# The first block of transposed x: two plain loads turned by TensorE instead of one, and the weight loads on one queue

## The chip, the cores and the metric

The kernel runs on one core of one Trainium2 chip. The metric is the device time of one execution in microseconds (us). One run in the set was taken with the hardware profiler; its trace gives every instruction with its start, its length and what it waited for, and the packets and landings of the DMAs.

## What is computed

The input x has 2048 rows (the sequence, S) of 512 columns (D), in bfloat16. Two mixers work on it, and a gate blends them:

```
g = sigmoid((x * gate_w).sum(-1))                       # one number a row
qkv = x @ wqkv                                          # 512 -> 3 * 512: q, k, v, 32 heads of 16
logits[s, w] = q[s] . k[s - 2 w] / 4,  w = 0..7         # sliding, dilated by 2; s - 2 w < 0 is masked
a = (softmax(logits) @ v[s - 2 w]) @ wo
h = layernorm(x)
b = (gelu(h^T @ w1 + b1) @ w2 + b2)^T                   # an MLP along the sequence: 2048 -> 1792 -> 2048
out = g * a + (1 - g) * b
```

What matters here is the very start: the product x @ wqkv, which needs x with its columns on the partitions, that is x transposed, and the layer norm, which needs x as it is.

## The kernel before, in words

**Layout.** x is kept twice. `X` holds it as it is, 16 tiles of 128 rows. `XT` holds it transposed: 4 parts of 128 columns (index d), each with 2048 entries along the sequence, which is worked on in 4 blocks of 512 rows. `WQKV` holds the weights as 4 parts of 128 rows (again d) by 1536 columns, q first, then k, then v. One projection is one of q, k, v for 128 of its 512 columns (index dl) and one block of 512 rows: four products, one for each d, that add up in one bank of PSUM (`f_proj`, line 614, products at L619). ScalarE copies the finished bank to SBUF (`f_evq`, L627 for q, L630 for k and v).

**The first block.** The eight projections of block 0 (q and k, four dl each) use all eight PSUM banks at once, and they are issued not projection by projection but part by part, as the parts of x and of the weights come in (the loop at lines 635 to 641): d = 0 of the four q, then d = 1, 2, 3 of the four q, then d = 0 and 1 of the four k, then d = 2 and 3 of the four k. So there are 32 products in a row, and then block 1 follows, q and k in turn, one projection after the other.

**How the transposed x arrives.** Three of the four parts of block 0 (384 columns) and all of the other blocks come by a transposing DMA (`ld_xt0`, L473, and `ld_xt`, L460). Part d = 0 of block 0 comes by a plain load of 512 rows by 128 columns (`d_xp`, line 479, issued through the helper at L429) into a borrowed buffer, `OUTS`. TensorE turns it by four products of 128 columns with an identity matrix (`f_tr`, L545), two of them into bank 5, two into bank 6; ScalarE copies bank 5 to `XT` (L555) and VectorE bank 6 (L557). The first four projections' products can start after both copies.

**Warm-up.** While the first loads are under way, TensorE multiplies constants (`f_warm`, L537): six products of 512 columns and one of 256 ahead of the turn, and one of 512 behind it.

**Queues.** SyncE (SP) issues nearly all loads, in the order of the program, ScalarE's queue (ACT) two of the first weight loads. Before: SP issues d_xp, the transposing DMA of 384 columns, the q weights for d = 2 and d = 3, the k weights for d = 0 and 1, those for d = 2 and 3, x tiles 0 and 1 (x0), the transposing DMA of block 1 (xt1), then x tiles 2 and 3 (x2), 4 to 7 (x4), blocks 2 and 3 (xt2, xt3), x8, x12, the v weights and the MLP's weights. ACT issues the q weights for d = 0 and d = 1. From x2 on, a load waits for the fifth load before it (`throttle`).

**Order of the work.** The kernel is planned when it is built: `_Sched` (line 72) simulates the engines with costs given by hand and fixes the order of each engine's instructions. For the first nine loads the time at which they are taken to land is written in by hand (`op_.lands`, line 487). The products of the projections are held in their order by `last_main`. VectorE's order is written out by hand (the `chain` at line 959): the indicator `rp`, the copy `ev_trb`, the layer norm's statistics of tiles 0 to 3 (`ln1_*`, L574), then the first products of q with shifted k (`qkm_0_0_0`, L690), and so on. The sums of those products over a head's columns are TensorE's, in two bursts of 64 products (`qkr_*`, L698). At the end of the kernel TensorE makes a @ wo (L878) and VectorE combines (L899).

## Time and profile before

| | |
|---|---|
| three runs | 167.96, 168.19, 168.55 us; median 168.19 us |
| the profiled execution | 168.55 us, its span 167.3 us |
| TensorE products | 860, busy 163.9 us (98% of the span) |
| VectorE | busy 151.3 us (90%) |
| ScalarE | busy 75.0 us (45%) |
| SyncE's DMA queue (q1) | 24.85 MB, 54.0% of 16 engines' span |
| ScalarE's DMA queue (q10) | 4.66 MB, 10.0% |
| first loads, from issue to landing | d_xp 3.1 us; q weights on ACT 3.0 us (median of two); transposing DMA of 384 columns 4.4 us; 128 KB weight loads on SP 3.0 us |

The span runs from the first instruction of the program to its last; the time of a run has 1.25 us more, which lie around the span. In the lists below, a line begins with start and length in us, or with a window; then come the engine (PE is TensorE's products, PEld its weight loads, DVE VectorE, ACT ScalarE, SP SyncE), the line of the kernel, the operation, what it writes and reads, its shape and how many such instructions were merged; in brackets, the idle time ahead of it and what ended it. `arena` is the whole of the kernel's SBUF, `ps` its PSUM. A product's shown length includes its way through the array, so products overlap: the pace is read from start to start.

### The profile page before, as it was taken

The page shows a single profiled execution, that of the slowest core. Times are in us where ns is not written, and L with a number is a line of the kernel's source. Part 1 is how long each engine was busy: PE and PEld are TensorE (multiplying, and loading weights), DVE is VectorE, ACT ScalarE, POOL GpSimd, SP SyncE. Part 2 cuts the span into 40 slices and gives each one's busy share as a digit, 9 for nine tenths or more (in the row PEclk, how much of TensorE's full clock was granted, in tenths as well). Part 3 has the DMA queues.
Part 4 walks back from the last instruction along what each step waited for, and adds up shares of the span by engine and source line. Part 5 has one row for each costly group of instructions (what it writes and reads, how often), then busy time and mean ns, then how long its engine had stood idle before and what let it go on. Part 6 is the DMA issues. An engine that isn't in the chain of part 4 may idle for free.

```text
span 167.3 us, 2152 instructions
## 1 busy us (share of the span) xinstructions
PE 163.9 (98%) x860; PEld 77.6 (46%) x860; DVE 151.3 (90%) x154; ACT 75.0 (45%) x116; POOL 0.7 (0%) x8
## 2 busy tenths in 40 slices
PE   7999999999999999999999999999999999999994
PEld 2455555554454444444444444444444444444463
DVE  0145999999999999999999999999999999999896
ACT  3077688889899818793113121131231321310100
POOL 1000000000000000000000000000000000000000
DMA  5999999968003837996579936462672580000454
GB/s 130 315 272 262 303 322 291 307 196 246 0 0 97 311 115 187 303 290 153 133 183 343 335 129 143 112 187 68 184 218 83 138 223 0 0 0 0 157 190 159
DMA packets 47625, 29.64 MB, mean 177 GB/s; under 512 B 9856, under 2 KB 46464, under 8 KB 47616
## 3 DMA queue, kind: packets, MB, share of 16 engines
q1 hardware_dynamic: 45504, 24.85, 54.0%
q10 hardware_dynamic: 2112, 4.66, 10.0%
q8 instruction: 7, 0.11, 0.3%
q14 instruction: 2, 0.02, 0.0%
HBM read 21.24 MB, written 2.10 MB: 140 GB/s over the span
## 4 chain that ended last, share of the span: by engine, by line
PE 94%; DVE 3%; DMA 2%; issue 0%
PE ps L812 29%; PE ps L862 29%; PE ps L619 25%; PE ps L878 6%; PE ps L698 4%; DVE arena L899 2%; DMA arena<-in_A_x_dram 2%; PE ps L545 0%; DVE arena L557 0%
## 5 line engine op out<-in xcount | busy, mean ns | idle before, releaser
L812 PE MATMUL ps<-arena 128*128 128x512 bf16 x224 | 48.7, 379 | 0.0
L862 PE MATMUL ps<-arena 128*128 128x512 bf16 x224 | 48.7, 379 | 0.0
L619 PE MATMUL ps<-arena 128*128 128x512 bf16 x192 | 42.3, 382 | 0.1
L690 DVE TENSOR_TENSOR arena<-arena 128x4096 bf16<-128x4096 bf16 (+1 forms) x12 | 35.5, 2996 | 2.3 <-ACT arena L630 1.8
L797 DVE TENSOR_TENSOR arena<-arena 128x8192 bf16<-128x8192 bf16 x8 | 35.0, 4419 | 0.0
L812 PEld LDWEIGHTS ps<-arena 128*128 128x128 bf16 x224 | 21.8, 98 | 26.7 <-ACT arena L728 0.4
L862 PEld LDWEIGHTS ps<-arena 128*128 128x128 bf16 x224 | 21.9, 98 | 26.5
L619 PEld LDWEIGHTS ps<-arena 128*128 128x128 bf16 x192 | 21.6, 114 | 20.8 <-DVE arena L557 0.7
L930 ACT ACTIVATE arena<-ps,arena 128x512 bf16<-128x512 f32 x16 | 12.4, 778 | 39.4 <-PE ps L862 39.4
L800 DVE TENSOR_TENSOR arena<-arena 128x4096 bf16<-128x4096 bf16 (+1 forms) x16 | 27.0, 1752 | 0.0
L630 ACT ACTIVATE arena<-ps 128x512 bf16<-128x512 f32 x32 | 18.5, 596 | 4.5 <-PE ps L619 4.5
L833 ACT ACTIVATE arena<-ps,arena 128x512 bf16<-128x512 f32 x14 | 9.6, 687 | 22.2 <-PE ps L812 17.4
L574 DVE BATCH_NORM_STATS2 arena<-arena 128x6 f32<-128x512 bf16 x16 | 10.0, 680 | 5.6 <-DMA arena<-in_A_x_dram 5.6
L878 PE MATMUL ps<-arena 128*128 128x512 bf16 (+1 forms) x80 | 14.2, 337 | 0.0
L899 DVE SCALAR_TENSOR_TENSOR arena<-ps,arena 128x512 bf16<-128x512 f32 (+1 forms) x20 | 11.5, 638 | 0.9 <-PE ps L878 0.7
L598 ACT ACTIVATE arena<-arena 128x512 bf16<-128x512 bf16 x16 | 12.2, 806 | 0.0
L627 ACT ACTIVATE arena<-ps 128x512 bf16<-128x512 f32 x16 | 9.0, 596 | 5.5 <-PE ps L619 5.4
L878 PEld LDWEIGHTS ps<-arena 128*128 128x128 bf16 x80 | 7.8, 98 | 6.3
L674 DVE SCALAR_TENSOR_TENSOR arena<-arena 128x512 bf16<-128x512 bf16 x16 | 10.1, 685 | 0.0
L744 DVE TENSOR_TENSOR arena<-arena 128x512 bf16<-128x512 bf16 (+4 forms) x11 | 7.3, 667 | 0.6 <-ACT arena L763 0.2
L698 PE MATMUL ps<-arena 128*32 128x512 bf16 x128 | 7.3, 380 | 0.0
L728 ACT ACTIVATE arena<-ps 128x512 bf16<-128x512 f32 x8 | 4.7, 592 | 4.6 <-PE ps L698 4.6
(42 smaller groups left out, 40.5 us busy)
## 6 DMA issues: line engine op xcount, KB each, us to landing
arena<-in_B_w_dram SPq DMA_DIRECT2D x7, 1024.0 KB, 8.3
arena<-in_B_w_dram SPq DMA_DIRECT2D x8, 896.0 KB, 5.1
arena<-arena ACTq DMA_DIRECT2D x32, 128.0 KB, 3.0
arena<-in_A_x_dram SPq DMA_DIRECT2D x4, 512.0 KB, 5.1
out_dram<-arena SPq DMA_DIRECT2D x14, 128.0 KB, 1.7
arena<-in_A_x_dram SPq DMA_DIRECT2D x1, 1536.0 KB, 7.9
arena<-in_A_wqkv_dram SPq DMA_DIRECT2D x2, 256.0 KB, 3.6
arena<-in_A_x_dram SPq DMA_DIRECT2D x2, 256.0 KB, 3.5
```

Of the source, the lines that this page charges most:

```text
L598: A("act", (lambda t_: (lambda e: e.activation(out=X[:, t_, :], in_=X[:, t_, :], func=AF.Identity, scale=col(RSTD, t_), bias=col(NMR, t_)) ...
L619: ins = e.matmul(ps[:, bank, s0:s1], lhsT=lhsT, rhs=XT[:, dt, sb * 512 + s0:sb * 512 + s1], start=(dt == 0 and s0 == 0), stop=(dt == 3))
L630: return lambda e: e.activation(out=dst, in_=ps[:, bank, :], func=AF.Copy)
L690: return lambda e: e.tensor_tensor(out=PBL[buf][:, :, 512 * c0:512 * (c0 + nc_)], in0=in0, in1=in1, op=ALU.mult)
L698: ins = e.matmul(ps[32 * c:32 * c + 32, 4 + wl, :], lhsT=RP, rhs=PBL[buf][:, wl, c * 512:(c + 1) * 512], start=(dl == 0), stop=(dl == 3), ...
L797: A("dve", (lambda o_, i0, i1: (lambda e: e.tensor_tensor(out=o_, in0=i0, in1=i1, op=ALU.mult)))(pv, in0, in1), 4.4, reads=v_res + ["atx_% ...
L800: A("dve", (lambda pv_, n__: (lambda e: e.tensor_tensor(out=pv_[:, 0:n__], in0=pv_[:, 0:n__], in1=pv_[:, n__:2 * n__], op=ALU.add)))(pv, n ...
L812: ins = e.matmul(ps[:, bank, :], lhsT=W1W[:, slot, st, 128 * e_:128 * e_ + 128], rhs=X[:, st, :], start=(st == 0), stop=(st == NST - 1))
L862: ins = e.matmul(ps[:, bank, :], lhsT=W2S[slot][:, ft, 128 * e_:128 * e_ + 128], rhs=UT[:, ft, :], start=(ft == 0), stop=(ft == NFT - 1))
L878: ins = e.matmul(ps[:, bank, 0:c1 - c0], lhsT=OT[:, t, 128 * i:128 * i + 128], rhs=WO[:, t, c0:c1], start=(t == 0), stop=(t == 3))
L899: A("dve", (lambda i_, b_, c0_, c1_: (lambda e: e.scalar_tensor_tensor(out=T1[:, i_, c0_:c1_], in0=ps[:, b_, 0:c1_ - c0_], scalar=col(G, i ...
L930: A("act", (lambda i_, bank_: (lambda e: e.activation(out=T1[:, i_, :], in_=ps[:, bank_, :], func=AF.Identity, scale=col(OMG, i_), bias=co ...
```

## The change

Two of the four parts of block 0 now come by plain loads. The borrowed buffer holds both (`xp0`, `xp1`), the second turn uses the same two banks, and its four products and two copies stand between the products of q for d = 0 and those of k for d = 0. The transposing DMA takes the other two parts, 256 columns instead of 384.

SP now issues all of the first loads: xp0, q weights for d = 0, k weights for d = 0, xp1, q and k weights for d = 1 in one load, the transposing DMA, q and k weights for d = 2, those for d = 3, xt1, and x0 behind xt1 instead of ahead of it. ACT issues none of them.

The order of the 32 products becomes: q d = 0 (4), the second turn, k d = 0 (4, in the bank order 4, 7, 5, 6), q and k d = 1 (8), q d = 2 (4), q d = 3 (4), k d = 2 and 3 (8). The warm-up is five products of 512 columns and one of 256 ahead of the first turn, and one of 512 and one of 256 behind it. VectorE's chain gets the second copy, `ev_trb1`, right behind the first. The planner's landing times are rewritten for the new loads.

```diff
-        XT0 = ["xt0_%d" % d for d in range(4)] + ["xt0_0b"]
+        XT0 = ["xt0_%d" % d for d in range(4)] + ["xt0_0b", "xt0_1b"]
...
-            dst = XT[:, 1:4, 0:512]
-            op = sch.dma("sp", lambda e: e.dma_start_transpose(dst, x2d[0:512, 128:512]), 512 * 384 * 2, ds, issue=1.25,
-                         writes=XT0[1:4], after=prev_dma(), name="d_xt0")
+            dst = XT[:, 2:4, 0:512]
+            op = sch.dma("sp", lambda e: e.dma_start_transpose(dst, x2d[0:512, 256:512]), 512 * 256 * 2, ds, issue=1.25,
+                         writes=XT0[2:4], after=prev_dma(), name="d_xt0")
...
-        XP = view("OUTS", BF16, [(128, 4), (1, 128)])
-        d_xp = sch.dma("sp", mk_dma(XP, xv[:, 0:4, 0:128]), 512 * 128 * 2, sch.dsem("xp"), writes=["outs0"], issue=0.4, name="d_xp")
...
-        first_loads = [ld_w(0, 0, 1, "act"), ld_xt0(), ld_w(0, 1, 1, "act"), ld_w(0, 2, 1), ld_w(0, 3, 1), ld_w(1, 0, 2), ld_w(1, 2, 2),
-                       ld_x(0, 2)]
+        XP = view("OUTS", BF16, [(512, 2), (128, 4), (1, 128)])
+
+        def ld_xp(dt):
+            op = sch.dma("sp", mk_dma(XP[:, dt], xv[:, 0:4, 128 * dt:128 * dt + 128]), 512 * 128 * 2, sch.dsem("xp%d" % dt),
+                         writes=["outs%d" % dt], after=prev_dma(), issue=0.4, name="d_xp%d" % dt)
+            init_dmas.append(op)
+            return op
+
+        def ld_qk(d):
+            ds = sch.dsem("wqk%d" % d)
+            op = sch.dma("sp", mk_dma(WQKV[:, d, 0:2 * D], wqkv_v[:, d, 0:2 * D]), 2 * 128 * D * 2, ds,
+                         writes=["wqkv0_%d" % d, "wqkv1_%d" % d], after=prev_dma(), issue=0.45, name="d_wqk%d" % d)
+            init_dmas.append(op)
+            return op
+
+        first_loads = [ld_xp(0), ld_w(0, 0, 1), ld_w(1, 0, 1), ld_xp(1), ld_qk(1), ld_xt0(), ld_qk(2), ld_qk(3)]
         ld_xt(1)
         first_loads.append(init_dmas[-1])
+        first_loads.append(ld_x(0, 2))
...
+        def turn(dt, prev):
+            for h in range(2):
+                lgr = ["lg%d_0" % (5 + h), "lg%d_1" % (5 + h)]
+                prev = A("pe", f_tr(dt, h), 0.215 if dt == 0 else 0.11, reads=["outs%d" % dt, "ident"], writes=lgr, after=[prev],
+                         name="tr%d%d" % (dt, h), prio=-100 if dt == 0 else 0)
+                dst = XT[:, dt, 256 * h:256 * h + 256]
+                pin = ps[:, 5 + h, 0:256]
+                if h == 0:
+                    A("act", (lambda d_, i_: (lambda e: e.activation(out=d_, in_=i_, func=AF.Copy)))(dst, pin), 0.35,
+                      reads=lgr, writes=["xt0_%d" % dt], name="ev_tra%d" % dt, prio=0)
+                else:
+                    A("dve", (lambda d_, i_: (lambda e: e.tensor_copy(out=d_, in_=i_)))(dst, pin), 0.35,
+                      reads=lgr, writes=["xt0_%db" % dt], name="ev_trb%d" % dt, prio=0)
+            return prev
...
-        A("pe", f_warm(6), 2.56, writes=["lg7_0", "lg7_1"], name="warm1", prio=-100)
+        A("pe", f_warm(5), 2.13, writes=["lg7_0", "lg7_1"], name="warm1", prio=-100)
...
+        w3_ = A("pe", f_warm(1, 256), 0.2, writes=["lg7_0", "lg7_1"], after=[tr_], name="warm4", prio=-100)
...
-        for (b0, d0, d1, s0, s1) in ((0, 0, 1, 0, 512), (0, 1, 2, 0, 512), (0, 2, 3, 0, 512), (0, 3, 4, 0, 512), (4, 0, 2, 0, 512), (4, 2, 4, 0, 512)):
-            for b in range(b0, b0 + 4):
+        for (bs, d0, d1, s0, s1) in ((range(4), 0, 1, 0, 512), ((4, 7, 5, 6), 0, 1, 0, 512), (range(8), 1, 2, 0, 512),
+                                     (range(4), 2, 3, 0, 512), (range(4), 3, 4, 0, 512), (range(4, 8), 2, 4, 0, 512)):
+            if bs == (4, 7, 5, 6):
+                last_main[0] = turn(1, last_main[0])
+            for b in bs:
...
-        chain(["rp", "ev_trb"] + ln1(0, 1, 2, 3) + ["qkm_0_0_0", "qkm_0_1_0"] + ln1(4, 5, 6, 7) + ln2(0)
+        chain(["rp", "ev_trb0", "ev_trb1"] + ln1(0, 1, 2, 3) + ["qkm_0_0_0", "qkm_0_1_0"] + ln1(4, 5, 6, 7) + ln2(0)
```

21 lines of the change are left out of this document (6 added, 15 removed).

## The prediction, on record before the changed kernel ran

> **What bounds the kernel now.** I read the chain that ended last first, then the first microseconds in order of time, then VectorE's waits, then the DMA rates of the first five microseconds. The chain in order of time (start, length, what):
>
> ```profile
> 0.80 3.10 DMA arena<-in_A_x_dram
> ...
> 4.04 0.60 PE ps L545 x4
> ...
> 4.66 0.44 DVE arena L557
> ...
> 5.15 33.44 PE ps L619 x152
> ...
> 161.68 3.98 DVE arena L899 x9
> ```
>
> From 5.15 us on the chain is TensorE alone, without a wait, up to the last output columns: 152 products in 33.44 us are 0.22 us each, and the tail behind TensorE (the last combine and its store) is the same whatever happens at the start. The 860 products are the time; only what lies ahead of 5.15 us, and work added to TensorE, can move the end. Ahead of it stands one path: the load d_xp (issued 0.80, landed 3.91), four small products that turn it (L545), ScalarE's and VectorE's copies of the result (L555, L557), then the first projection at 5.15, that is 1.24 us after the landing.
>
> TensorE's pace in these microseconds, by its weight loads in order of time:
>
> ```profile
> 2.07 0.15 PEld L537 LDWEIGHTS ps<-const-bfloat16-1.0 128*128 128x128 bf16 x1 [0.28 <-issue]
> 2.50 0.15 PEld L537 LDWEIGHTS ps<-const-bfloat16-1.0 128*128 128x128 bf16 x1 [0.28 <-issue]
> ...
> 5.14 0.15 PEld L619 LDWEIGHTS ps<-arena 128*128 128x128 bf16 x2 [0.68 <-DVE arena L557]
> 5.56 0.15 PEld L619 LDWEIGHTS ps<-arena 128*128 128x128 bf16 x1 [0.27 <-issue]
> 5.98 7.95 PEld L619 LDWEIGHTS ps<-arena 128*128 128x128 bf16 x37 [0.28 <-issue]
> ```
>
> The reader is to see two paces: 0.43 us a product of 512 columns at first, and 7.95/37 = 0.215 us later. The products start at 5.15, 5.56, 5.98, 6.26, 6.48: the third took 0.28 us, so 0.13 us of it at the slow pace, and the switch fell at about 6.11 us. The windows view gives the granted clock as 1.00 throughout, so I go by the pace.
>
> DMA in windows (busy time of each engine, then granted clock, DMA share, GB/s):
>
> ```profile
> 1.90:2.20 0.30, 0.30 (x2) 0.13 (x1) 0.00 (x0) 0.30 (x1) 0.00 (x0) 1.00 0.22 53
> 2.20:2.60 0.40, 0.40 (x3) 0.12 (x2) 0.00 (x0) 0.40 (x1) 0.00 (x0) 1.00 0.61 116
> 2.60:3.00 0.40, 0.40 (x3) 0.12 (x2) 0.00 (x0) 0.40 (x1) 0.00 (x0) 1.00 1.01 312
> 3.00:3.40 0.40, 0.40 (x3) 0.07 (x1) 0.00 (x0) 0.13 (x1) 0.00 (x0) 1.00 1.20 329
> 3.80:4.80 1.00, 0.76 (x5) 0.45 (x5) 0.14 (x1) 0.35 (x1) 0.00 (x0) 1.00 1.27 279
> ```
>
> A slow start, then full engines. Up to 3.4 us, where d_xp's last packet starts, 319 KB moved, of which d_xp is 131 KB; the rest went to the two weight loads on ScalarE's queue. d_xp shared the engines while they were full.
>
> VectorE, in order of time:
>
> ```profile
> 9.08 1.29 DVE L574 BATCH_NORM_STATS2 arena<-arena 128x6 f32<-128x512 bf16 x2 [3.99 <-DMA arena<-in_A_x_dram]
> 11.95 1.29 DVE L574 BATCH_NORM_STATS2 arena<-arena 128x6 f32<-128x512 bf16 x2 [1.59 <-DMA arena<-in_A_x_dram]
> 15.08 4.49 DVE L690 TENSOR_TENSOR arena<-arena 128x4096 bf16<-128x4096 bf16 x2 [1.84 <-ACT arena L630]
> ...
> 30.68 6.68 DVE L690 TENSOR_TENSOR arena<-arena 128x4096 bf16<-128x4096 bf16 x3
> ```
>
> The q·k products start at 15.08 on ScalarE's copy, not on a load, and run dense to 37.36. TensorE's burst that reads them (L698) starts at 38.52: VectorE is 1.16 us early there.
>
> **The change part by part**, against the profiled run: span 167.3, time 168.55, so 1.25 us around the span, which stays. That run is the highest of the three (167.96, 168.19, 168.55).
>
> *Loads.* The first eight loads are 1.57 MB before and after: xp1's 131 KB and 512 packets of 256 bytes leave the transposing DMA. With ScalarE's queue empty, xp0 has the engines alone. By 2.6 us the two windows moved 53 x 0.3 + 116 x 0.4 = 62 KB; granting xp0 all of that, its other 69 KB at 279 GB/s (the window in which nearly all packets were 256 bytes) take 0.25 us: last packet at 2.85 instead of 3.4, landing 0.55 us sooner, at 3.35. Bounds: 2.9, if the full rate holds from the first packet (1.92 + 131/279 + the 0.5 us from last packet to landing); 3.91, if the slow start is xp's own and company cost it nothing. I take 3.35: of the three it alone uses the rates as measured. The Trainium skill, "DMA: Bandwidth & Descriptors", section on queues, rings and completion order, says that an engine takes its queue rows in turn, packet by packet; the shared windows agree, and by that rule alone the landing is also sooner, not at 3.91.
>
> wq0 moves from ScalarE's queue (0.80) to second on SP's: issued about 1.29, and at the row's 2.9 us it lands at 4.2, behind xp0 and before the first projection. The same SP issues of 0.44 us put wk0 at 1.78, xp1 at 2.27, wqk1 at 2.75, the transposing DMA at 3.25. Its issue took 1.64 us for 384 columns; for 256 I take 1.25 (bounds 1.1 in proportion, 1.64). Then wqk2 4.55, wqk3 5.05, xt1 5.55 (5.58 before). xp1 is to land by 5.3 (2.27 + 3.1), wanted at 6.2 by the second turn, and all of TensorE stands behind that wait; xt0 by 7.6 (4.4 us after issue, as before), wanted at 9.1; wqk3 by 8.9 (8.39 before for the same bytes, issued 0.5 later), wanted at 10; xt1 at 11.04 or sooner, wanted at 12.5. Each has 0.9 us or more of cover.
>
> *TensorE's start.* 3.35 + 1.24 = 4.59 instead of 5.15. The warm-up is one 512-column product shorter ahead of the turn (it ends near 3.13) and 256 columns longer behind it: 0.21 us, from 0.71 to 0.92 us after the landing, inside the 1.24 us that the copies take. Cost nothing.
>
> *Second turn.* Four more products of 128 columns on the path. At the slow pace they took 0.38 us (4.04 to 4.42); the 256-column products at the end stand 0.11 us apart, so at full pace 128 columns are at least 0.055. I take 0.06 each, 0.24 in sum (bounds 0.22 and 0.43). Two copies (0.38 on ScalarE, 0.42 on VectorE) fall where both engines are idle, ScalarE until its next copy (8.62 before), VectorE until x0 lands. k's products come in bank order 4, 7, 5, 6, so that banks 5 and 6 are read out meanwhile: from the second turn's start to TensorE going on was 0.77 us before, at full pace about 0.68; TensorE wants bank 5 after 3 x 0.06 + 2 x 0.2155 = 0.61. Wait 0.07; I take 0.05 (bounds 0 and 0.11).
>
> *Sum.* Four products from 4.59 at the slow pace start at 4.59, 5.00, 5.42, 5.85; the switch at 6.11 leaves 0.39 of the fourth, 0.08 us; it ends at 6.19. Plus 0.24 and 0.05: the fifth product at 6.48. Before, the fifth started at 6.48. **In the profiled run the change is worth nothing**: half of the 0.56 us is lost since the early products run at half pace, the other half pays for the second turn. Had the switch come before 4.59, the gain would be 0.56 - 0.29 = 0.27.
>
> The Trainium skill, "TensorE: Matmul & The Clock Gate", part 1, says that the clock is halved until a busy window of about 3.4 us has passed, that the window runs freely and that the count of slow products so varies by run. The trace agrees in kind (0.43, then 0.215 us, switch at 6.11); one run cannot show that it varies.
>
> The three runs spread by 0.59 us; a switch at 6.11 costs (6.11 - 5.15)/2 = 0.48 against an early one, so the spread may be this (an inference). A median run then lies between both cases: 0 to -0.27. I take -0.1 from the median 168.19: **168.1**.
>
> *Moved load x0.* It goes from ahead of xt1 to behind it, and x2 and x4 one place back: x0 issued near 8.85, where x2 stood (landed 11.93), x2 near 9.45, where x4 stood (13.74, for twice the bytes). VectorE's statistics of x0 end by 13.24, those of x2 by 14.5, at x4's landing by 15.05: before 15.08. q's products of block 0 now end later against k's, so ScalarE's eight copies (0.48 us apart) bunch up: from their start 2.17 us before block 1's first product, with q's and k's copy of block 1 behind them, the q·k product starts 2.76 us after that product, not 2.56. 0.2 us late, under 1.16 us of cover. Later loads go back by some 0.6 us; xt2 (landed 15.78, wanted near 19.4) and the rest have more.
>
> **The rivals.** *A, faster, 167.5:* xp0 lands at 2.9 to 3.1 and the clock is up early, perhaps because warm-up, turn and projections leave fewer pauses (0.48 and 0.30 us before). Start 0.8 to 1.0 earlier, less 0.29: -0.6 from the median. For it: the path to the first projection hangs on this one load; against: the 53 GB/s with which the stream begins before the ScalarE queue's packets come. Chance 0.20.
>
> *B, it does not do what it says, 168.5:* xp0 lands at 3.91 again because the slow start is its own; the second turn and its wait are paid, 0.29. For it: 53 GB/s while alone; against: 312 GB/s shared. Chance 0.12, still within 0.3%.
>
> *C, slower, 168.95:* x2 lands too late. Place: VectorE's chain ahead of the first q·k product. Point: start later than 15.08 + 1.16 = 16.24, so x2 later than 16.24 - 1.29 = 14.95; beyond it TensorE's burst waits one for one. If x2 came at 15.78 (where xt2 landed), products start at 17.1, 0.85 us too late: 168.1 + 0.85. For it: SP's issue of xt1 took 3.25 us and everything behind hangs on it; against: x4's 512 KB in nearly that place landed at 13.74. Chance 0.13, and a burst that the planner's new order puts too early belongs here.
>
> **How the numbers follow.** 0.3% (0.5 us) is about what a measurement of this kernel can tell from no change. Forecast 168.1 at 0.55 and B at 0.12 are within it: 0.67. A: faster, 0.20. C: slower, 0.13. Range: from 167.5 (A's value) to 168.8 (B with the turn at the slow pace, 0.43, and 0.11 for the banks: 168.73), leaving out C's end and the far end of A.
>
> **What would show it.** Right: xp0 landing near 3.35 and the first projection near 4.6; L545 eight times; no pause over 0.1 us on TensorE up to the last product; VectorE's first L690 still waiting on ScalarE. Wrong: xp0 at 3.9; a pause before the fourth or sixth group of products; L690 or L698 released by a load or VectorE; a switch of pace well ahead of 5.5 us.

## The result, and the profile after

The changed kernel took 168.89 us (median of 22 runs, 168.47 to 169.89), the kernel before 168.34 us on the same chip (22 runs, 167.94 to 168.87). The ratio is 1.0039 (95% interval 1.0027 to 1.0051): **slower by 0.55 us**. Predicted were 168.1 (167.5 to 168.8) and, as the likeliest case, no change that can be measured.

The profiled execution took 168.74 us, its span 167.5 us (before: 168.55 and 167.3). Its chain of work, in order of time:

```profile
0.84 2.50 PE ps L546 x6
3.34 0.54 PE ps L554 x4
3.88 0.64 PE ps L546 x2
4.52 1.77 PE ps L638 x4
6.29 0.43 PE ps L554 x4
6.72 6.40 PE ps L638 x29
```

The load is gone from the chain's head: TensorE is the chain from the first warm-up product on. xp0 landed at 3.16 us and the first turn starts at 3.29; the warm-up products, by their shown lengths, reach up to it, so the load does not show. TensorE's products in order of time (start, length):

```profile
4.40 1.89 PE L638 MATMUL ps<-arena 128*128 128x512 bf16 x4
6.09 0.63 PE L554 MATMUL ps<-arena 128*128 128x128 bf16 x4
6.51 3.36 PE L638 MATMUL ps<-arena 128*128 128x512 bf16 x14
```

The first projection starts at 4.40 instead of 5.15, the second turn begins at 6.09, and the fifth product comes at 6.51, where before it came at 6.48. The pace switches at 6.87 (before 6.11). Block 1's first product is at 12.74 (before 12.52), the last product of the kernel starts at 165.07 (before 164.86). So this one execution is 0.2 us slower, without a pause that a load ends; it alone would not explain the 0.55 us of the medians.

VectorE, in order of time:

```profile
12.98 2.47 DVE L593 BATCH_NORM_STATS2 arena<-arena 128x6 f32<-128x512 bf16 x4 [5.80 <-DMA arena<-in_A_x_dram]
15.37 4.48 DVE L712 TENSOR_TENSOR arena<-arena 128x4096 bf16<-128x4096 bf16 x2
```

The q·k products (L712) start at 15.37 instead of 15.08, with no idle time ahead of them: they stand behind the four statistics, which stand behind x0. TensorE's burst on them (L720) starts at 38.73, the products it needs end at 37.64: 1.09 us of cover left, of 1.16.

DMA in three windows, first of the kernel before and then of the changed one (busy time of PE, PEld, DVE, ACT, POOL with counts, granted clock, DMA share, GB/s):

```profile
2.90:4.90 2.00, 1.73 (x8) 0.60 (x6) 0.24 (x1) 0.61 (x2) 0.00 (x0) 1.00 1.23 301
4.90:6.90 2.00, 1.91 (x7) 0.78 (x7) 0.19 (x1) 0.00 (x0) 0.00 (x0) 1.00 1.09 296
6.90:8.90 2.00, 2.00 (x11) 1.07 (x10) 0.00 (x0) 0.28 (x1) 0.00 (x0) 1.00 1.12 312
```

```profile
2.90:4.90 2.00, 2.00 (x10) 0.80 (x9) 0.42 (x1) 0.38 (x1) 0.00 (x0) 1.00 0.95 239
4.90:6.90 2.00, 2.00 (x9) 0.92 (x8) 0.14 (x1) 0.36 (x1) 0.00 (x0) 1.00 1.13 210
6.90:8.90 2.00, 2.00 (x11) 1.08 (x10) 0.28 (x1) 0.03 (x1) 0.00 (x0) 1.00 1.40 281
```

This is the line that the rest hangs on. In these 6 us the engines moved 301, 296, 312 GB/s before and 239, 210, 281 after: 2 x (62 + 86 + 31) = 358 KB less (some of it, about 50 KB, had moved by 2.9 us already). The same bytes come over the same sixteen engines, but later. It is not this one pair of profiles alone: up to 8.9 us the changed kernel moved 1572 to 1685 KB in four profiles; the kernel before moved 1969 KB, and four runs below that keep its queues (e4, f4, f6, l2) 1791 to 1917 KB. The page's list of DMA issues says it too: the weight loads of 256 KB on SP's queue took 4.4 us from issue to landing, where before they took 3.6.

```profile
arena<-in_A_wqkv_dram SPq DMA_DIRECT2D x3, 256.0 KB, 4.4
```

Three more profiles of the changed kernel, taken later (h1, h2, h3), show how the landings vary. "Wanted" is worked out for the earliest case that these profiles show: first projection at 4.29, full pace of 0.2155 us a product, 0.36 us for the second turn.

| landing, us | before | predicted | changed | h1 | h2 | h3 | wanted |
|---|---|---|---|---|---|---|---|
| xp0 | 3.91 | 3.35 | 3.16 | 2.95 | 2.96 | 3.04 | |
| xp1 | | 5.3 | 4.75 | 4.93 | 4.87 | 5.69 | 5.15 |
| weights d = 1 (q and k) | 4.31 (q), 7.44 (k) | | 6.48 | 6.93 | 6.52 | 6.37 | 6.4 |
| transposing DMA | 5.73 | 7.6 | 7.52 | 7.96 | 7.55 | 7.39 | 8.1 |
| weights d = 2 | 6.11 (q), 8.39 (k) | | 9.13 | 8.85 | 8.97 | 9.04 | 8.1 |
| weights d = 3 | 6.45 (q), 8.39 (k) | 8.9 | 9.82 | 10.22 | 9.61 | 9.69 | 9.0 |
| xt1 | 11.04 | 11.04 or sooner | 11.74 | 12.14 | 11.54 | 11.62 | 11.55 |
| x4 | 13.74 | | 15.44 | 15.96 | 16.58 | 15.35 | |
| xt3 | 17.73 | | 19.40 | 19.84 | 21.01 | 19.72 | |
| switch of pace | 6.11 | | 6.87 | 5.43 | 6.59 | before 4.29 | |

The column "before" is one profile, and an early one: in e4, f4, f6 and l2, with the same queues, the last weights landed at 8.12, 9.10, 9.58 and 8.67, and xt3 at 18.97, 18.51, 18.90 and 19.16. What differs more is the need. In the order of before, the last weights (k's for d = 2 and 3) are wanted behind 24 products, at 5.15 + 24 x 0.2155 = 10.32 even at full pace; the changed order wants all of d = 2 at 8.1 and all of d = 3 at 9.0.

### The profile page after: what moved, and what is told of

The parts are those of the page before. It is cut to its first block, busy times and chain, and to the rows that moved or that the text cites. A ratio compares the mean times of both kernels' runs of the same rounds, so it can differ in the third digit from the quotient of the medians.

```text
span 167.5 us, 2148 instructions
## 1 busy us (share of the span) xinstructions
PE 163.5 (98%) x850; PEld 78.2 (47%) x864; DVE 151.5 (90%) x155; ACT 75.1 (45%) x117; POOL 0.7 (0%) x8
## 4 chain that ended last, share of the span: by engine, by line
PE 96%; DVE 2%; issue 1%
PE ps L884 29%; PE ps L834 29%; PE ps L638 25%; PE ps L900 6%; PE ps L720 4%; DVE arena L921 2%; PE ps L546 2%; PE ps L554 1%
## 5 line engine op out<-in xcount | busy, mean ns | idle before, releaser
L712 DVE TENSOR_TENSOR arena<-arena 128x4096 bf16<-128x4096 bf16 (+1 forms) x12 | 35.5, 2997 | 0.4 <-PE ps L720 0.4
L649 ACT ACTIVATE arena<-ps 128x512 bf16<-128x512 f32 x32 | 18.8, 599 | 3.5 <-PE ps L638 3.4
L646 ACT ACTIVATE arena<-ps 128x512 bf16<-128x512 f32 x16 | 9.3, 603 | 5.2 <-PE ps L638 5.2
L720 PE MATMUL ps<-arena 128*32 128x512 bf16 x128 | 7.3, 380 | 0.0
L750 ACT ACTIVATE arena<-ps 128x512 bf16<-128x512 f32 x8 | 4.7, 592 | 4.6 <-PE ps L720 4.6
```

The source lines that it names most:

```text
L649: return lambda e: e.activation(out=dst, in_=ps[:, bank, :], func=AF.Copy)
L712: return lambda e: e.tensor_tensor(out=PBL[buf][:, :, 512 * c0:512 * (c0 + nc_)], in0=in0, in1=in1, op=ALU.mult)
L720: ins = e.matmul(ps[32 * c:32 * c + 32, 4 + wl, :], lhsT=RP, rhs=PBL[buf][:, wl, c * 512:(c + 1) * 512], start=(dl == 0), stop=(dl == 3), ...
```

## The experiments

The theories, with the letters that the expectations use. **L**: the first loads come later from one queue, and TensorE waits for them, in the executions in which the pace switches early. **R**: the second turn is the cost, by its four products, its wait for xp1 and its wait for banks 5 and 6. **W**: the thinner warm-up makes the switch of pace later. **C** (in the first four) is the prediction's rival: x0 and x2 come late and hold up VectorE's first q·k product. **P** and **Q** came up later and are both forms of L: by P, the transposing DMA's place between plain loads slows them; by Q, one sequencer issuing all loads does. Each ratio is against the kernel before, run beside it on the same chip, with its 95% interval; the times are medians, and a ratio is not that of the medians: a few high runs move it more. Where an edit moves loads, the planner's hand-written landing times change with them; the cuts below leave that out.

### e1, e2, e3, e4: one part of the change at a time

**e1** puts x0 ahead of xt1 again, in the changed kernel.

```diff
-first_loads = [..., ld_qk(2), ld_qk(3)]
+first_loads = [..., ld_qk(2), ld_qk(3), ld_x(0, 2)]
 ld_xt(1)
-first_loads.append(ld_x(0, 2))
```

> The changed kernel with the load x0 put ahead of xt1 again; all else as changed. Three theories stand for the 0.55 us by which the changed kernel is slower (168.89 against 168.34). Theory W (the switch of TensorE's pace from 0.43 to 0.215 us a product comes later): no change, 168.7 to 169.1. Theory C (the late x0 and x2 hold up VectorE's first q.k product, at 15.37 instead of 15.08 in the changed kernel's profile, and a burst behind it): back to 168.2 to 168.5. Theory R (the second turn's four products and their copies cost it): no change, 168.7 to 169.1.

Measured: 168.71 (168.17 to 169.12, 12 runs), 1.0017 (1.0004 to 1.0030). In its profile the pace switches at 5.14; TensorE waits for the banks (0.31 and 0.24 between products) and then from 8.35 to 9.07 for the weights of d = 2, landed 8.94; block 1 waits once more, to 12.64, for xt1 (landed 12.50), which now stands behind x0. x0's place may be worth 0.2 us; it is not the loss (l2, below, finds nothing).

**e2** gives the changed kernel the six warm-up products of before.

```diff
-        A("pe", f_warm(5), 2.13, ...)
+        A("pe", f_warm(6), 2.56, ...)
```

> The changed kernel with six products of 512 columns ahead of the first turn, as before, instead of five. The warm-up then ends near 3.56, behind the landing of xp0 at 3.16, so the first projection starts 0.3 us later than at 4.40. Theory W: the switch of pace comes sooner by more than that, 168.3 to 168.7. Theories C and R: the later start costs 0 to 0.3 us, 168.9 to 169.2.

Measured: 168.88 (168.56 to 169.38), 1.0030 (1.0016 to 1.0045). The first projection comes later, at 4.68, and already at full pace. Nothing is won, as TensorE now waits three times: to 6.96 (weights d = 1 landed 6.92), to 8.99 (d = 2, 8.86) and to 10.13 (d = 3, 10.08). The first projection starts 0.4 us later than in h1, and block 1 starts at 12.75, where h1 has 12.89: the loads set the time. Against W, for L.

**e3** takes out xp1 and the second turn; the transposing DMA takes 384 columns again, ahead of the weights of d = 1, all of it on SP.

```diff
...
-first_loads = [ld_xp(0), ld_w(0, 0, 1), ld_w(1, 0, 1), ld_xp(1), ld_qk(1), ld_xt0(), ld_qk(2), ld_qk(3)]
+first_loads = [ld_xp(0), ld_w(0, 0, 1), ld_w(1, 0, 1), ld_xt0(), ld_qk(1), ld_qk(2), ld_qk(3)]
...
-            if bs == (4, 7, 5, 6):
-                last_main[0] = turn(1, last_main[0])
```

> The changed kernel without the second load and the second turn: the transposing DMA brings 384 columns as before, ahead of the weights for d = 1. Loads on SP only, the early xp0, the changed warm-up and the changed order of the products stay. Theory R: 168.1 to 168.5, as fast as before or faster. Theory W: the slow pace lasts as long as in the changed kernel, but 0.25 to 0.43 us of small products go: 168.4 to 168.7. Theory C: 168.8 to 169.1.

Measured: 169.14 (168.88 to 169.89, 8 runs), 1.0047 (1.0029 to 1.0066): slower still, without any second turn. TensorE's weight loads in order of time:

```profile
5.14 0.98 PEld L638 LDWEIGHTS ps<-arena 128*128 128x128 bf16 x5 [0.26 <-issue]
8.19 2.31 PEld L638 LDWEIGHTS ps<-arena 128*128 128x128 bf16 x12 [2.07 <-issue]
```

An idle time of 2.07 us ahead of 8.19; the load of d = 1 landed at 8.09. (The release is given as "issue"; the landing 0.1 us earlier fits.) In the changed kernel these weights landed at 6.48, so the edit made a load later as it took the turn out. It shows that a late load alone costs as much; it does not price the turn.

**e4** gives the kernel before the changed warm-up.

```diff
-        A("pe", f_warm(6), 2.56, ...)
+        A("pe", f_warm(5), 2.13, ...)
...
-        w3_ = tr_
+        w3_ = A("pe", f_warm(1, 256), 0.2, ..., after=[tr_], name="warm4", prio=-100)
```

> The kernel before with nothing but the changed warm-up: five products of 512 columns and one of 256 ahead of the turn, one of 512 and one of 256 behind it. Theory W, if the warm-up is what moves the switch: slower than before by 0.3 to 0.6 us, 168.6 to 168.9, with the switch of pace later than 6.11. Theories C and R: as before, 168.2 to 168.5.

Measured: 168.60 (168.06 to 170.36, 12 runs), 1.0028 (0.9998 to 1.0057). Three of the runs took 169.9 to 170.36. In the profile TensorE pauses for 0.74 us ahead of the turn and switches at 6.27. Not clear by itself; k1, below, shows an execution in which a pause in the warm-up goes with a late switch.

### f1, f4, f5, f6: queues, warm-up, and the price of four small products

**f1** issues the weights of d = 2 and 3 on ScalarE's queue, behind ScalarE's first copy.

```diff
-first_loads = [..., ld_xt0(), ld_qk(2), ld_qk(3)]
+first_loads = [..., ld_xt0(), ld_qk(2, "act"), ld_qk(3, "act")]
...
+        chain(["ev_tra0", "d_wqk2", "d_wqk3", "ev_tra1"])
```

> The changed kernel with one difference: the weight loads for d = 2 and d = 3 (256 KB each) are issued by ScalarE, right behind its first copy (about 4.1 and 4.6 us), instead of by SP behind the transposing DMA. Theory L (loads: on SP's one queue the weights for d = 2 and 3 land at 9.13 and 9.82 in the changed kernel's profile, and TensorE waits for them in every run whose pace switches early): they land by 8 us, xt1 an issue or two sooner, and the time falls to 168.2 to 168.6. Theory W (the pace switches late): no change, 168.7 to 169.1. Theory R (four small products and the wait for banks 5 and 6): no change, 168.7 to 169.1.

Measured: 169.57 as the median of the five runs below 171 us (all eight: 168.77 to 173.12), 1.0092 (1.0056 to 1.0129), the opposite of what was expected. In its one profile (171.69 us, 2 us above that median, so no measure of the others) the two loads took 7.7 us from issue to landing, and the transposing DMA landed at 11.41, not 7.5; TensorE waits from 8.76 to 11.45. That the three got in each other's way is likely from this; why, and whether it is so in the faster runs, is not shown.

**f4** makes the warm-up of the kernel before denser.

```diff
-        A("pe", f_warm(6), 2.56, ...)
+        A("pe", f_warm(7), 2.99, ...)
...
-        w3_ = tr_
+        w3_ = A("pe", f_warm(1, 256), 0.2, ..., after=[tr_], name="warm4", prio=-100)
```

> The kernel before with the pauses of its warm-up filled: seven products of 512 columns ahead of the turn instead of six (they end at the landing of d_xp), and 256 columns more behind it. Theory W: a denser warm-up lets the pace switch sooner or at least narrows the spread of the runs, 168.0 to 168.3, none above 168.8. Theory L: nothing moves, 168.2 to 168.5, since the loads of the kernel before land ahead of their use either way.

Measured: 168.38 (168.10 to 168.87, 11 runs), 1.0007 (0.9994 to 1.0020); switch at 5.68. No gain; that the kernel before switches early in its median run anyway would explain it, but is not shown.

**f5** is the kernel before with one turn, but all first loads on SP and the changed warm-up.

```diff
-first_loads = [ld_w(0, 0, 1, "act"), ld_xt0(), ld_w(0, 1, 1, "act"), ld_w(0, 2, 1), ...
+first_loads = [ld_w(0, 0, 1), ld_xt0(), ld_w(0, 1, 1), ld_w(0, 2, 1), ...
```

> The kernel before with ScalarE's two weight loads put on SP (behind d_xp, and behind the transposing DMA), and the changed kernel's warm-up; one turn only, 384 columns by the transposing DMA, everything else in the order of before. d_xp lands near 3.1 and the first projection starts near 4.4, as in the changed kernel; no second turn is paid. Theory L: the transposing DMA is third in its queue, not sixth, so the weights keep their times within 0.5 us; 168.0 to 168.4. Theory W: the pace switches as late as in the changed kernel, 168.3 to 168.8. Theory R: 168.0 to 168.3.

Measured: 168.88 (168.38 to 169.36, 12 runs), 1.0032 (1.0018 to 1.0046). TensorE's weight loads:

```profile
5.13 0.15 PEld L618 LDWEIGHTS ps<-arena 128*128 128x128 bf16 x1 [0.28 <-issue]
6.32 2.31 PEld L618 LDWEIGHTS ps<-arena 128*128 128x128 bf16 x12 [1.04 <-DMA arena<-in_A_x_dram]
9.16 1.44 PEld L618 LDWEIGHTS ps<-arena 128*128 128x128 bf16 x8 [0.54 <-DMA arena<-in_A_wqkv_dram]
```

The first projection comes at 4.29, 0.86 us early, and then TensorE waits for weights that land at 6.21 and at 9.12. Block 1 waits a third time, to 12.84, for xt1, which landed at 12.71 (it stands behind x0 here, as before). No theory's forecast was met: L had taken the weights to keep their times. But without second turn and new bank order the same 0.5 us are lost, and in this profile it is a landing that sets the start of block 1. (The changed warm-up is in it too; e4 does not settle what that costs.) (The trace names x for the first wait; of the two loads that it needed, x came at 5.55 and the weights at 6.21.)

**f6** adds four products of 128 columns, whose result nobody uses, to the kernel before, behind its first four projections' products.

```diff
+            if d0 == 1:
+                for h_ in range(2):
+                    last_main[0] = A("pe", f_tr(h_), 0.11, ..., after=[last_main[0]], name="tx%d" % h_)
             for b in range(b0, b0 + 4):
```

> The kernel before with four more products of 128 columns behind the first four of the projections, at the place of the second turn, their result not used and not copied. This prices the second turn's products alone. Theory R: the whole of 0.3 to 0.55 us, 168.7 to 168.9. Theory L: 0.2 to 0.3 us, 168.55 to 168.7, less where TensorE waits for a load anyway.

Measured: 168.55 (168.21 to 169.12), 1.0017 (1.0004 to 1.0030): 0.16 us by the medians (168.39 beside it); in the profile the four stand 0.055 apart, 0.22 in sum. That is R's sure part, 0.16 to 0.22 us.

### g1, g2: without the loads, and with the loads as before

**g1** doesn't load the q and k weights of d = 2 and 3 (512 KB) and uses those of d = 1 in their place.

```diff
-first_loads = [..., ld_xt0(), ld_qk(2), ld_qk(3)]
+first_loads = [..., ld_xt0()]
...
+                    dw = min(dt, 1) if tn < 2 else dt
```

> The changed kernel without the loads of q's and k's weights for d = 2 and d = 3 (512 KB): the weights for d = 1 are used in their place, so the output is that of other weights; every product is still done. Theory L (TensorE waits for these loads, at 9.13 and 9.82 in the changed kernel's profile): the time falls by most of what the change cost, to 168.1 to 168.5, and the lowest runs lie near 167.8. Theories W (late switch of the pace) and R (second turn): no change, 168.7 to 169.0, the lowest near 168.5.

Measured: 168.19 (167.74 to 168.77, 12 runs), 0.9996 (0.9980 to 1.0012). The loss is gone. TensorE's products:

```profile
4.29 1.05 PE L639 MATMUL ps<-arena 128*128 128x512 bf16 x4
5.18 0.39 PE L554 MATMUL ps<-arena 128*128 128x128 bf16 x4
5.40 1.15 PE L639 MATMUL ps<-arena 128*128 128x512 bf16 x4
6.88 3.00 PE L639 MATMUL ps<-arena 128*128 128x512 bf16 x13 [0.32 <-DMA arena<-in_A_wqkv_dram]
```

At full pace from 4.29, second turn 0.22 us, the bank wait, then one wait for the weights of d = 1 (landed 6.83), the only late load left. From 6.88 on 24 products of 0.2155 us lead to block 1 at 12.05. The last product, 164.41, less the 152.33 us from block 1 to it (the same in both kernels' first profiles) gives 12.08: the account closes. Two limits: the loads behind the missing ones come sooner as well (xt1 at 9.80, xt3 at 17.57), so g1 shows that the loads are the loss, not which of them; and the early start pays for the second turn in it.

**g2** gives the changed kernel the queues, the order of loads and the warm-up of before; the second turn stays.

```diff
-first_loads = [ld_xp(0), ld_w(0, 0, 1), ld_w(1, 0, 1), ld_xp(1), ld_qk(1), ld_xt0(), ld_qk(2), ld_qk(3)]
+first_loads = [ld_xp(0), ld_w(0, 0, 1, "act"), ld_w(1, 0, 1, "act"), ld_xt0(), ld_xp(1), ld_qk(1), ld_qk(2), ld_qk(3), ld_x(0, 2)]
...
```

> The changed kernel with the loads in the queues and the order of before: ScalarE issues q's and k's weights for d = 0, SP issues xp0, then the transposing DMA (256 columns), then xp1, the weights for d = 1, 2 and 3, x0, xt1; warm-up as before. The second turn and the changed order of the products stay. Theory L: the loads land as before, the first projection starts at 5.15 again, and what is left is the second turn's products (0.2 us as measured alone) and up to 0.1 for the banks: 168.5 to 168.7, the lowest runs near 168.2. Theory R: 168.7 to 169.0. Theory W: 168.3 to 168.5.

Measured: 168.91 (168.45 to 169.73), 1.0035 (1.0020 to 1.0050): where R had put it, above L's 168.5 to 168.7. The loads are on time again (weights d = 3 at 8.43, xt3 at 17.73), and its profile (168.81, switch at 5.96) shows no wait for one; but xp1, now behind the transposing DMA, lands at 6.08. That would make the second turn wait in executions that switch early. No such execution was profiled, so this is an inference, and some 0.2 us of g2's 0.58 stay unexplained. Of all runs this one fits L worst.

### h1, h2, h3: three more looks at the changed kernel

> The changed kernel as it is, profiled once more, to see whether the late switch of the pace (6.87 in its first profile) is its own or chance. Theory L: the switch falls anywhere between 4 and 7.5 us; where it is before 6, TensorE shows a wait of 0.3 to 0.8 us ahead of the products that need the weights for d = 2. Theory W: the switch comes after 6.3 again and TensorE waits for no load.

> The changed kernel a third time, for the same question. Theory L: a switch between 4 and 7.5 us, with a wait for the weights for d = 2 where it is early. Theory W: a switch after 6.3 and no such wait.

> The changed kernel once more, for a fourth profile. Its slowest runs lie 1 us above its median; in one profile TensorE waited 0.82 us for block 3 of the transposed x (xt3), which landed at 21.0. Theory L: xt3 lands between 19.4 and 21 and TensorE waits for it where it is after 20.5. Otherwise the slow runs have another cause.

Measured: 168.98, 169.49 and 168.64 us. The switch came at 5.43, near 6.59, and before 4.29; with 6.87 in the first profile that is two times later and two times earlier than before's 6.11, so W falls as a constant cost of the change. h1's weight loads:

```profile
6.46 0.27 PEld L638 LDWEIGHTS ps<-arena 128*128 128x128 bf16 x2 [0.41 <-ACT arena L566]
6.98 1.44 PEld L638 LDWEIGHTS ps<-arena 128*128 128x128 bf16 x8 [0.25 <-DMA arena<-in_A_wqkv_dram]
8.95 0.58 PEld L638 LDWEIGHTS ps<-arena 128*128 128x128 bf16 x4 [0.53 <-issue]
10.26 1.66 PEld L638 LDWEIGHTS ps<-arena 128*128 128x128 bf16 x9 [0.73 <-DMA arena<-in_A_wqkv_dram]
```

The reader is to see four waits: for a bank, then for the weights of d = 1 (landed 6.93), of d = 2 (8.85, though the row says "issue") and of d = 3 (10.22). From 10.3 twelve products are left, 12 x 0.2155 = 2.59: block 1 at 12.89. The last product, 165.22 less 152.33, gives 12.89. So in this execution the last weights' landing sets the time, and nothing ahead of it matters. h3's products:

```profile
4.29 1.05 PE L638 MATMUL ps<-arena 128*128 128x512 bf16 x4
5.74 0.40 PE L554 MATMUL ps<-arena 128*128 128x128 bf16 x4 [0.40 <-DMA arena<-in_A_x_dram]
5.97 2.88 PE L638 MATMUL ps<-arena 128*128 128x512 bf16 x12
9.17 0.60 PE L638 MATMUL ps<-arena 128*128 128x512 bf16 x2 [0.33 <-DMA arena<-in_A_wqkv_dram]
```

Full pace from the first projection on: the second turn waits for xp1 (landed 5.69), and TensorE again at 9.17 for the weights of d = 2 (9.04). Sixteen products from 9.17 lead to 12.62; 164.96 less 152.33 gives 12.63. In h2 the switch is late, and the loads at the front are in time; the wait comes later:

```profile
17.73 2.75 PE L638 MATMUL ps<-arena 128*128 128x512 bf16 x12
21.14 3.19 PE L638 MATMUL ps<-arena 128*128 128x512 bf16 x14 [0.66 <-ACT arena L646]
```

xt3 landed at 21.01, and the first product of block 3 starts at 21.14, 0.13 us later, the same distance as from xp's landing to the first turn before (3.91, 4.04). The trace names ScalarE, but the projections go through four banks in turn, and its copy that ended at 21.12 was of the projection just before: the row is misread if it is taken at its word. From 20.11, the start before it, to 21.14 are 1.03 us where 0.2155 were due, so 0.82 are lost. Eight of the changed kernel's 22 runs took 169.29 us or more, and none of the 22 beside them over 168.87; a wait for xt3 would explain them, but h2 (169.49) is the only execution of that length that was profiled.

### k1, k2, k3: which property of the queue

**k1** is the kernel before with ScalarE loading its table first and then issuing two q weight loads; the q weights of d = 0 go second on SP.

```diff
-first_loads = [ld_w(0, 0, 1, "act"), ld_xt0(), ld_w(0, 1, 1, "act"), ld_w(0, 2, 1), ...
+pre = A("act", ..., name="pre", prio=-100)
+first_loads = [ld_w(0, 0, 1), ld_xt0(), ld_w(0, 1, 1, "act"), ld_w(0, 2, 1, "act"), ...
...
+first_loads[2].order.add(pre)
+first_loads[3].order.add(first_loads[2])
...
-        A("pe", f_warm(6), 2.56, ...)
+        A("pe", f_warm(5), 2.13, ...)
```

> The kernel before with an early start and nothing else of the change: ScalarE loads its table first (a copy of one constant column stands ahead), then issues q's weights for d = 1 and 2 at about 2.2 and 2.7 us; SP issues d_xp, q's weights for d = 0, the transposing DMA of 384 columns, and the rest as before, with as many issues as before. Warm-up as changed. One turn. Theory L (what counts is when the later loads land): d_xp near 3.1, first projection near 4.4, k's weights by 9 and xt3 by 18.2; the time is 168.0 to 168.4. If the early start itself were the harm, 168.6 to 168.9.

Measured: 169.72 (168.98 to 170.47, 6 runs), 1.0082 (1.0050 to 1.0114); the expectation was missed. The edit did not do what it was meant to: ScalarE issued its loads while the table was still loading, at 0.86 and 1.29 us and not at 2.2 and 2.7, so they ran beside xp again.

```profile
0.80 1.28 ACT L483 ACT_TABLE_LOAD   x1 [0.80 <-PEq L1041]
0.86 0.97 ACTq L429 DMA_DIRECT2D arena<-in_A_wqkv_dram  x2
```

The early start, which k1 was to test, did not come about. xp landed only at 4.00, so that the shorter warm-up left a pause of 1.0 us, and TensorE's weight loads then show half pace to the end of the front:

```profile
2.50 0.15 PEld L540 LDWEIGHTS ps<-const-bfloat16-1.0 128*128 128x128 bf16 x1 [0.28 <-issue]
4.11 0.35 PEld L548 LDWEIGHTS ps<-arena 128*128 128x128 bf16 x4 [1.46 <-issue]
...
8.23 0.15 PEld L622 LDWEIGHTS ps<-arena 128*128 128x128 bf16 x1 [0.28 <-issue]
8.65 1.92 PEld L622 LDWEIGHTS ps<-arena 128*128 128x128 bf16 x9 [0.28 <-issue]
```

Idle times of 0.28 us between weight loads are the pace of 0.43 us; they go on to 8.65, and the switch came at 8.82. So W may have a true core: here a pause of 1.0 us in the warm-up goes with a switch 2.7 us later than in the profile before. It is one execution, and with pauses of 0.74 us (e4) and 0.83 us (k2) the profiled ones switched at 6.27 and 5.42.

**k2** is the changed kernel with the weights of d = 0, q and k, on ScalarE's queue.

```diff
-first_loads = [ld_xp(0), ld_w(0, 0, 1), ld_w(1, 0, 1), ...
+first_loads = [ld_xp(0), ld_w(0, 0, 1, "act"), ld_w(1, 0, 1, "act"), ...
```

> The changed kernel with one difference: q's and k's weights for d = 0 are issued by ScalarE at 0.8 and 1.3 us instead of by SP. The transposing DMA stays behind the weights for d = 1. Theory Q (loads are late since one queue issues them all): the weights for d = 3 land by 8.8, xt3 by 18.3, the time falls to 168.5 to 168.7. Theory P (loads are late since the transposing DMA stands between plain loads instead of near the front): the weights for d = 3 land after 9.4, xt3 after 19, 168.8 to 169.1.

Measured: 169.82 (168.61 to 170.74, 6 runs), 1.0086 (1.0053 to 1.0118). Neither forecast was met. The first weights did come sooner (d = 3 at 8.91), but xt3 only at 20.07, and xp0 later, at 3.83. The profiled execution was the fastest, 168.61, and switched early, at 5.42; it shows the pause ahead of the turn, but not what it did in the others:

```profile
2.07 1.27 PE L547 MATMUL ps<-const-bfloat16-1.0 128*128 128x512 bf16 x3
3.96 0.58 PE L555 MATMUL ps<-arena 128*128 128x128 bf16 x4 [0.62 <-DMA arena<-in_A_x_dram]
```

**k3** puts the transposing DMA second on SP, as before, with all loads on SP.

```diff
-first_loads = [ld_xp(0), ld_w(0, 0, 1), ld_w(1, 0, 1), ld_xp(1), ld_qk(1), ld_xt0(), ld_qk(2), ld_qk(3)]
+first_loads = [ld_xp(0), ld_xt0(), ld_w(0, 0, 1), ld_w(1, 0, 1), ld_xp(1), ld_qk(1), ld_qk(2), ld_qk(3)]
```

> The changed kernel with one difference: the transposing DMA is second on SP, right behind xp0, ahead of the weights; all loads stay on SP. q's weights for d = 0 are issued near 2.7 instead of 1.3, so the first projection starts near 5.3. Theory P: the weights for d = 3 land by 8.8, xt3 by 18.3, 168.5 to 168.8. Theory Q: the weights for d = 3 land after 9.4, xt3 after 19, 168.9 to 169.3.

Measured: 169.88 (169.74 to 170.63, 4 runs), 1.0103 (1.0072 to 1.0134). The first projection waits to 5.52, the weights of d = 3 land at 9.92, xt3 at 20.78. TensorE waits 0.94 us more for the weights of d = 1 (landed 8.62, first product 8.67), and then no more. The loads are as late with the transposing DMA in its old place, which speaks for Q and against P; but the edit also issues the first weights later, by 1.4 us.

### l1, l2: two queues without the pause, and x0's place alone

**l1** is k2 with seven warm-up products instead of five.

```diff
-first_loads = [ld_xp(0), ld_w(0, 0, 1), ld_w(1, 0, 1), ...
+first_loads = [ld_xp(0), ld_w(0, 0, 1, "act"), ld_w(1, 0, 1, "act"), ...
...
-        A("pe", f_warm(5), 2.13, ...)
+        A("pe", f_warm(7), 2.99, ...)
```

> The changed kernel with q's and k's weights for d = 0 issued by ScalarE, and seven products of 512 columns ahead of the turn instead of five, which fill the pause of 0.83 us that the later landing of xp0 (3.83) had left ahead of the turn in the same kernel without them (median 169.82, from 168.61 to 170.74). If that pause made its runs slow and spread (a switch of the pace put off by a pause in the warm-up), the median falls to 168.5 to 168.9 and the spread to under 1.2 us. If its runs were slow through late loads (block 3 of x near 20.0), it stays at 169.4 or more.

Measured: 168.59 (168.16 to 168.89, 12 runs), 0.9998 (0.9970 to 1.0027); beside it before took 168.29 (167.94 to 170.27, 23 runs, three of them above 169.3). TensorE's products:

```profile
2.07 2.12 PE L547 MATMUL ps<-const-bfloat16-1.0 128*128 128x512 bf16 x5
3.99 0.63 PE L555 MATMUL ps<-arena 128*128 128x128 bf16 x4
5.14 1.05 PE L639 MATMUL ps<-arena 128*128 128x512 bf16 x4
```

No pause ahead of the turn, and 1.2 us less than k2 in the median: the warm-up was what made k2 slow, as expected of the pause. That it worked through a late switch is not shown, since no slow execution of k2 was profiled. The weights of d = 2 and 3 land at 8.01 and 9.08, and TensorE waits for no load, only for the banks (0.32 and 0.24 between products). 5.14 + 32 x 0.2155 + 0.36 = 12.40; 164.76 less 152.33 gives 12.43. By the medians l1 is 0.3 us above before, about the second turn's 0.36; the interval, widened by before's three high runs, does not tell that from none.

**l2** is the kernel before with x0 behind xt1.

```diff
-first_loads = [..., ld_w(1, 2, 2), ld_x(0, 2)]
+first_loads = [..., ld_w(1, 2, 2)]
 ld_xt(1)
+first_loads.append(ld_x(0, 2))
```

> The kernel before with x0 put behind xt1, as in the change, and nothing else. Theory L with its tail (blocks 2 and 3 of the transposed x come late since more plain loads stand ahead of them): xt3 lands after 18.5 instead of 17.73, the time rises by 0 to 0.2 us, 168.3 to 168.5. If the moved x0 is what costs most of the change's 0.55 us, 168.7 or more. If it costs nothing, 168.2 to 168.4 with xt3 before 18.3.

Measured: 168.41 (167.88 to 168.90, 12 runs), 1.0004 (0.9979 to 1.0029). The moved load alone costs nothing that can be measured, though xt3 comes at 19.16 with it. Its profile (168.27 us) shows what the kernel before does with an early switch: the pace switches at 5.35, TensorE waits for no load, and block 1 starts at 12.16.

## Why the prediction was wrong, point by point

**The loads: the step that failed.** The prediction took each load's time from issue to landing as it was before and added the later issue, and found that "Each has 0.9 us or more of cover." Two things were wrong in it. The landings: the weights of d = 3 came at 9.61 to 10.22 in four profiles, not at 8.9, and "Later loads go back by some 0.6 us" was 1.6 to 2.8 us for x4 and 1.7 to 3.3 for xt3 (part of this is that the profile before had early landings). xt1 came at 11.54 to 12.14, not by 11.04. And the yardstick: the wanted times were read from the one slow front with its switch at 6.11. In an early one TensorE asks for the weights of d = 2, which the prediction did not list, at 8.1, when they land at 8.85 to 9.13; even by the prediction's own way (issued 4.55, plus the 3.6 us of a 256-KB load before) they would land at 8.15, with no cover.

So "Had the switch come before 4.59, the gain would be 0.56 - 0.29 = 0.27" is turned round. An early switch gains at most 0.1 us after the change: in h1, h3 and e2 the next landing ends TensorE's run, and block 1 starts at 12.89 and 12.63 in h1 and h3, where the first profile, with its late switch, has 12.74. The kernel before has no such wait in its profile and would reach block 1 at 5.15 + 32 x 0.2155 = 12.05 if it ran at full pace throughout; l2's profile reaches it at 12.16. That is 0.5 to 0.7 us. L is shown from both sides: without the late loads the loss is gone (g1), with the late loads and no second turn it is there (f5, e3), and with the loads sooner and no pause, what is left by the medians is about the second turn (l1). g2 does not fit without a wait for xp1 that no profile shows.

**xp0 and the start: right, a little better than forecast.** Landing at 3.16 (3.35 predicted, bounds 2.9 and 3.91) and 2.95 to 3.04 later; the first projection 1.24 us after the landing, as taken (1.24 to 1.34 in four profiles). Rival B, xp0 at 3.9 again, did not happen here, but it did in k1 and k2 (4.00 and 3.83), where ScalarE's queue took part again.

**The second turn: within its bounds, the banks just over.** In the first profile it ran at the slow pace and cost 0.43, its upper bound. At full pace it costs 0.22 (f6, g1). For the banks 0.05 was taken, with a bound of 0.11; the two gaps of 0.31 and 0.24 where two of 0.2155 were due are 0.12. TensorE gets bank 5 0.75 us after the second turn's start (h1: 5.71 to 6.46), not 0.68.

**The working in the profiled run: close, in part by luck** ("worth nothing"; it lost 0.2). The fifth product came at 6.51 for 6.48 since two errors cancelled: the start was 0.19 sooner than taken, and the switch came at 6.87 instead of 6.11, so that all four products and the turn ran at the slow pace. It was also the least telling execution, since a late switch hides late loads.

**Moved load x0: the cost right, the wait not.** The q·k products start 0.29 us later (0.2 was taken) and the cover holds at 1.09 us; l2 finds no cost. But VectorE's first L690 (now L712) was to wait still on ScalarE's copy, and it stands directly behind the statistics of x0 and x2. Rival C had the right kind, a load that comes too late, in the wrong place: it put it at VectorE's statistics, and the wait is TensorE's own, for weights and, in h2, for xt3.

**The pace.** The rule of the Trainium skill, "TensorE: Matmul & The Clock Gate", part 1, that the count of slow products varies by run, agrees with the four profiles of the changed kernel (6.87, 5.43, 6.59, before 4.29).

**What stays open.** Why loads issued by SP alone come later. The trace shows SP's issues at 0.42 to 0.58 us for each plain load and 1.3 to 5.1 us for a transposing DMA, one after the other, and the rates of 210 to 239 GB/s while they go on. That the engines ran short of work is not shown: their busy share in the three windows is 0.95, 1.13 and 1.40, in the mean 1.16 against 1.15 before, so only the first window speaks for it. P and Q are not told apart either: k3 is no clean test, k2's late xt3 (20.07) does not fit Q, and g2, with two queues and the transposing DMA near the front, has the earliest landings (8.43 and 17.73), but one profile each does not outweigh a spread from 8.12 to 9.58 with the queues of before. Also open: f1's landings, and 0.2 us of g2.

None of the versions that make all the loads beats the kernel before by more than the noise.

## What to carry to other kernels

Judge the cover of a load against the fastest timetable that its consumer can have, not against the one that a single profile shows; here the switch of pace moves that timetable by about 1 us between executions (the fifth product at 5.40 in g1, at 6.51 in the changed kernel's first profile). An earlier start is worth only as much as the next loads allow: list each of them with its landing and the time at which it would then be wanted, down to the last. A change of the order moves what is wanted as much as a change of the queue moves what lands. And when loads are gathered on one queue, check whether the same bytes land later: read the GB/s by windows before and after, in more than one profile of each.

## What was not expected of the hardware

- Plain loads of 256-byte rows (xp0, 131 KB) landed 2.15 to 2.40 us after issue where all first loads were on SP; with ScalarE's loads issued beside them they took 2.9 to 3.2, over all runs here.
- The sixteen parts of one load do not land together. In the changed kernel's first profile thirteen parts of the weights of d = 2 landed between 8.11 and 8.18 us, the other three at 8.81, 8.86 and 9.13; in h2 fifteen by 8.28 and one at 8.97. TensorE waits for the last.
- A pause of 1.0 us in the warm-up (k1) went with a switch of pace at 8.82 us, and closing one of 0.83 us (k2 to l1) took 1.2 us off the median; yet k2's own profile, with its pause, switched at 5.42.
- The products' pace halves and doubles (0.43 and 0.2155 us for 512 columns) while the granted clock stands at 1.00 throughout, so that column does not show it.
- A transposing DMA of 256 columns beside plain weight loads on the other queue landed at 11.41 instead of 7.52, in the one execution of 171.69 us that was profiled (f1).
- ScalarE issued two DMAs at 0.86 and 1.29 us while its table load ran from 0.80 to 2.08 (k1).
